# Block-sparse attention and a feed-forward layer in one kernel: q, k and v handed over in the operands' layout

## The chip, the cores and the metric

The kernel runs on one core of a Trainium2 chip. The metric is the device time of one execution in microseconds (us). Before the change three runs took 1019.51 us in the median (1017.39 to 1022.18).

## What is computed

The reference is attention over blocks of 32 positions with a mask, followed by a layer of the feed-forward kind (FFN). There are 4 batches of 8 heads, 768 positions and a head dimension of 64.

```python
scores = scale * np.matmul(q, k.transpose(0, 1, 3, 2))
# a pair of blocks is allowed when it is within the window, in a first or last row or column, or sampled
scores = np.where(mask, scores, -1000000000.0)
scores = scores - np.max(scores, axis=-1, keepdims=True)
attn = np.exp(scores)
attn = attn / (np.sum(attn, axis=-1, keepdims=True) + 1e-09)
x = np.matmul(attn, v)          # heads side by side: 3072 tokens of 512
h = x @ w_in                    # 512 to 2048
g = h - np.tanh(h)
out = g @ w_out                 # 2048 to 512
```

## The kernel before

**Precision.** Every float32 operand of a product is split into a high part that TensorE takes in its reduced float32 form and a low part that is the rest, and a product is the sum of three products of parts.

**The attention** goes over 16 pairs of heads (`pr`), two heads `h` of a pair, and six tiles of 128 keys (`kt`) of each head, so over 192 key tiles. For each pair, k and q are loaded in the order of the reference, with 128 partitions of positions (`load`, line 123). TensorE must contract over the head dimension, so `prep_qk` (line 178) transposes them: 6 transposes of 128x128 for k and 6 for q (line 186) into a buffer `pt` in PSUM. ScalarE copies the high part `hi` out of it (line 188), and VectorE subtracts it from the transposed values, which gives the low part `lo` (line 189). `dist` (line 192) then spreads the parts by DMA into one of three slots, 12 transfers for a pair (line 201). A slot holds four operands of the scores: sA (high k, mask, ones), sB (high q, one-hot blocks, minus the row maximum), sC (low k over high k) and sD (high q over low q).

For each key tile there are two products. `smax` (line 238) makes approximate scores `sm` from the high parts (line 245), and VectorE reduces them to row maxima `mc` (line 246). After six of them `smax_fin` (line 248) transposes the maxima on TensorE (`pmt`, line 251), VectorE turns them into `nm` (line 253), and a DMA writes `nm` as the last row of sB (line 254). `qk_exp` (line 263) then makes the scores `st` in full (lines 269 and 270; line 270 reads the row of `nm`), and ScalarE takes the exponential `pe` (line 272). `split` (line 275) splits it into `ph` (ScalarE, line 282, one in twelve on VectorE) and `pl` (GpSimd, line 284, one in twelve on VectorE). `accum` (line 288) multiplies them with v (lines 299, 305 and 306, 18 short products for a tile). `prep_v` (line 208) scales and splits v: VectorE finds its largest value (line 212), ScalarE writes the high part (line 230), VectorE the low one (line 231). `norm` divides by the row sums, and `spill` writes the result of a pair to DRAM.

`sm`, `st` and `pt` share three PSUM buffers (`big`), and `pmt`, `av` and the small transposes of `prep_v` share two (`one`).

**The order.** Each step is entered in a list with a time in key tiles (`at`, line 332) and emitted in the order of these times. `TQK = -15.1` puts the preparation of k and q 15.1 tiles ahead of the pair's first `st`, `TSM = -10.3` puts `smax` 10.3 tiles ahead. This order is only a priority. A list scheduler then sets the order on each engine, and takes a later step first where the one ahead of it isn't ready by its own reckoning. On the chip each engine, and SP's queue of DMA issues, works strictly in the order that came out.

**The first pair** goes the same way as the others: load, transposes, copies, 12 transfers. `fill` (line 169) writes mask and one-hot rows into the slots by DMA. `urgent` and `after` keep less urgent transfers behind those of the first pair.

**The FFN** (class `FFN`, line 441) goes over chunks of tokens and 16 tiles of the 2048 hidden columns. Its weights lie in DRAM as 64-bit floats; `convert` (line 411) makes float32 of a tile by three VectorE instructions (lines 415, 418, 421). The first three tiles of both weights are fetched and converted during the attention (`load_pre` and `convert_pre`, lines 358 and 364, at times `W0 + DW * x`) and go back to DRAM.

## Time and profile before

| what | us |
|---|---|
| three runs, median (range) | 1019.51 (1017.39 to 1022.18) |
| span of the profiled execution | 1019.9 |
| its start, up to the first product `st` of full scores | 27.98 |
| pair 0, from there to the first `st` of pair 1 | 29.91 |
| pair 1 | 36.19 |
| pairs 2 to 14 (13 pairs) | 320.92 |
| pair 15, to the end of its last `st` | 18.40 |
| the rest: last `accum` and FFN | 586.50 |

The profile gives no time of the profiled execution besides its span, which lies within the three runs. In the profile PE is TensorE's products and PEld its weight loads, DVE is VectorE, ACT ScalarE, POOL GpSimd, SP the queue that issues the DMAs. A row of the timeline has the start and the length in us, the engine, the line of the kernel, the operation and the tiles it writes and reads. PEclk is the clock that TensorE was granted, as a share of the full one.

### The profile page before, as it was taken

What the parts mean: (1) busy time and instruction counts of PE and PEld (TensorE: products, weight loads), DVE (VectorE), ACT (ScalarE), POOL (GpSimd) and SP (SyncE); (2) the same over time, 40 slices, a digit from 0 to 9 for tenths busy, and PEclk for the clock granted to TensorE, in tenths of its full rate; (3) what the DMA queues carried; (4) which work ended last, traced back from release to release, by engine and by line L of the source; (5) the groups of instructions that cost most, each with busy time, mean ns of one, the idle gap of its engine ahead of it and who ended that gap; (6) DMA issues with size and microseconds to landing.
All of it is one profiled execution on the core that took longest, in us unless ns stands there. A gap on an engine that the chain in (4) does not pass through costs nothing.

```text
span 1019.9 us, 19428 instructions
## 1 busy us (share of the span) xinstructions
PE 948.4 (93%) x7472; PEld 795.2 (78%) x7472; DVE 786.0 (77%) x1261; ACT 590.9 (58%) x926; POOL 637.0 (62%) x436
## 2 busy tenths in 40 slices
PE   5888999999999999897888899999999999999997
PEld 3667877888788888785766678888888888888896
DVE  5689887878788888979899987666666756666676
ACT  1665887888888888744344444445444534543453
POOL 1564777777778777866877866545455544544554
PEclk9997999999999999999899999999999999999999
DMA  7987687777766757133233121011000100000010
GB/s 193 252 223 205 144 175 151 157 173 169 159 157 156 156 131 183 48 120 105 81 114 92 43 93 52 1 42 42 21 5 17 63 1 1 31 11 1 1 42 22
DMA packets 73549, 97.75 MB, mean 96 GB/s; under 512 B 5880, under 2 KB 63416, under 8 KB 73456
## 3 DMA queue, kind: packets, MB, share of 16 engines
q1 hardware_dynamic: 73456, 96.51, 37.4%
q8 instruction: 59, 0.97, 0.4%
q14 instruction: 34, 0.28, 0.1%
HBM read 43.59 MB, written 14.16 MB: 57 GB/s over the span
## 4 chain that ended last, share of the span: by engine, by line
PE 64%; DVE 18%; DMA 8%; issue 5%; ACT 2%; POOL 1%; SPq 1%; POOLq 0%; DVEq 0%; ACTq 0%
PE h L507 21%; PE o L545 7%; PE o L543 7%; PE o L544 7%; PE st L269 5%; PE sm L245 5%; PE st L270 4%; DMA slot<-hiq 4%; PE av L299 2%; DVE g L524 2%; PE av L306 2%; PE av L305 2%; DMA slot<-nm 2%; DVE rs L316 2%; DVE mc L246 2%
## 5 line engine op out<-in xcount | busy, mean ns | idle before, releaser
L284 POOL TENSOR_TENSOR pl<-pe,ph 128x768 f16<-128x768 f32 x173 | 294.8, 1721 | 132.6 <-ACT ph L282 98.1
L530 POOL TENSOR_TENSOR gl<-g,gh 128x512 fp32r<-128x512 f32 (+2 forms) x112 | 135.1, 1209 | 191.6 <-ACT gh L529 191.3
L246 DVE TENSOR_REDUCE mc<-sm 128x1 f32<-128x768 f32 x192 | 181.6, 950 | 49.6 <-PE sm L245 48.4
L272 ACT ACTIVATE pe<-st 128x768 f32<-128x768 f32 x192 | 154.4, 805 | 77.3 <-PE st L270 72.8
L529 ACT ACTIVATE gh<-g 128x512 fp32r<-128x512 f32 (+2 forms) x112 | 63.9, 571 | 219.8 <-DVE g L526 210.6
L520 POOL TENSOR_SCALAR mk<-u 128x512 f32<-128x512 f32 (+2 forms) x112 | 160.9, 1436 | 46.6 <-ACT u L514 39.8
L522 DVE TENSOR_TENSOR g<-h,u 128x512 f32<-128x512 f32 (+2 forms) x112 | 68.4, 611 | 127.1 <-ACT t L516 115.8
L269 PE MATMUL st<-slot 128*128 128x512 f32 (+1 forms) x384 | 145.4, 379 | 8.8 <-DVE mc L246 4.8
L282 ACT ACTIVATE ph<-pe 128x768 f16<-128x768 f32 x168 | 141.7, 843 | 4.5
L270 PE MATMUL st<-slot 89*128 89x512 f32 (+1 forms) x384 | 128.7, 355 | 4.9 <-DMA slot<-nm 4.9
L299 PE MATMUL av<-vhl,ph 128*128 128x65 f16 x1152 | 130.2, 195 | 0.6 <-DVE sc L220 0.6
L245 PE MATMUL sm<-slot 88*128 88x512 f32 (+1 forms) x384 | 114.6, 385 | 16.7 <-DMA slot<-hiq 12.5
L305 PE MATMUL av<-vhl,ph 128*128 128x64 f16 x1152 | 130.0, 196 | 0.0
L306 PE MATMUL av<-vhl,pl 128*128 128x65 f16 x1152 | 128.2, 194 | 0.1
L306 PEld LDWEIGHTS <-pl 128*128 128x128 f16 x1152 | 107.9, 100 | 10.8 <-issue 6.8
L299 PEld LDWEIGHTS <-ph 128*128 128x128 f16 x1152 | 108.3, 98 | 4.6 <-issue 1.1
L305 PEld LDWEIGHTS <-ph 128*128 128x128 f16 x1152 | 108.9, 98 | 2.3 <-issue 1.6
L543 PE MATMUL o<-wx,gh 128*128 128x512 f32 x240 | 96.0, 400 | 7.9 <-ACT gh L529 6.9
L507 PE MATMUL h<-slot,wx 128*128 128x384 f32 (+1 forms) x480 | 102.5, 363 | 0.5 <-DVE t L523 0.5
L269 PEld LDWEIGHTS st<-slot 128*128 128x128 f32 x384 | 76.0, 198 | 28.9 <-DVE mc L246 7.4
L545 PE MATMUL o<-wx,gl 128*128 128x512 f32 x240 | 92.0, 398 | 4.9 <-POOL gl L530 4.7
L514 ACT ACTIVATE u<-h 128x512 f32<-128x512 f32 (+2 forms) x112 | 59.7, 533 | 62.8 <-PE h L507 52.4
(108 smaller groups left out, 2021.8 us busy)
## 6 DMA issues: line engine op xcount, KB each, us to landing
slot<-hik SPq DMA_DIRECT2D x64, 192.0 KB
slot<-hiq SPq DMA_DIRECT2D x64, 192.0 KB
stage<-w_in SPq DMA_DIRECT2D x13, 512.0 KB
stage<-w_out SPq DMA_DIRECT2D x13, 512.0 KB
rawk<-k SPq DMA_DIRECT2D x16, 384.0 KB
rawq<-q SPq DMA_DIRECT2D x16, 384.0 KB
slot<-lok SPq DMA_DIRECT2D x32, 192.0 KB
slot<-loq SPq DMA_DIRECT2D x32, 192.0 KB
```

Source lines behind the costliest of these rows:

```text
L245: nc.tensor.matmul(pm[:, c], lhsT=sB[s][0:88, j, t * P : (t + 1) * P], rhs=sA[s][0:88, j, c], start=True, stop=True)
L246: nc.vector.tensor_reduce(out=mcs[h][:, t : t + 1], in_=pm[:, 0:S], op=ALU.max, axis=AX.X)
L269: nc.tensor.matmul(st[:, c], lhsT=sC[s][:, j, kc], rhs=sD[s][:, j, c], start=True, stop=False)
L270: nc.tensor.matmul(st[:, c], lhsT=sA[s][0:89, j, kc], rhs=sB[s][0:89, j, c], start=False, stop=True)
L284: d = eng.tensor_tensor(out=pl, in0=pe, in1=ph, op=ALU.subtract)
L299: m = nc.tensor.matmul(o[:, to, :], lhsT=ph[:, c], rhs=vv[:, 0:65], start=(kt == 0 and t == 0), stop=False, skip_group_check=True)
L305: nc.tensor.matmul(o[:, to, 0:64], lhsT=ph[:, c], rhs=vv[:, 65:129], start=False, stop=False, skip_group_check=True)
L306: nc.tensor.matmul(o[:, to, :], lhsT=pl[:, c], rhs=vv[:, 0:65], start=False, stop=last, skip_group_check=True)
L507: nc.tensor.matmul(ph, lhsT=w[:, cc], rhs=x[:, c, tk], start=(k == 0), stop=(k == 3 * NCT - 1))
L520: nc.gpsimd.tensor_scalar(out=mk, in0=u, scalar1=THR2, scalar2=None, op0=ALU.is_gt)
L543: nc.tensor.matmul(o, lhsT=gh[:, c], rhs=wo[0][ft], start=(ft == 0), stop=False)
L545: nc.tensor.matmul(o, lhsT=gl[:, c], rhs=wo[0][ft], start=False, stop=(ft == NFT - 1))
```

## The change

- numpy now hands over k and q with the head dimension on the partitions, the two heads of a pair side by side and the two halves of 384 positions on the upper and lower 64 partitions. v comes with 128 positions on the partitions. The loads are plain copies of 128 rows of 768 values, as many bytes as before.
- `prep_qk` has no transposes and no PSUM buffer: ScalarE copies `hi` from the loaded tile, and VectorE subtracts `hi` from the loaded tile. `dist` is as it was, for pairs 1 to 15.
- Positions stand in natural order, so the table `TORD` is gone, and output rows are written in order.
- The first pair's operands are no longer spread by `dist`. `load_first` loads k and q of pair 0 twice, on both halves of the partitions (8 transfers of 192 KB). `first_high` and `first_low` write the slot's parts by ScalarE (8 copies), GpSimd and VectorE (2 subtractions each). Mask and one-hot rows of the first slot are written by VectorE (head 0) and GpSimd (head 1). The small constants come through ScalarE's DMA queue, and so do the rows `nm` of heads 0 and 1.
- The first weights have later times: `W0` goes from 40 to 52, the step `DW` from 24.7 to 23.5, and the conversion from 4 to 12 key tiles behind its load.

```diff
-W0, DW = 40, 24.7
+W0, DW = 52, 23.5
...
     def load(pr, which="kqv", first=None):
-        b, hp = divmod(pr, H // 2)
-        r = loads.setdefault(pr, [])
+        r = loads.setdefault(pr, {})
         for nm, src in ((n, x) for n, x in (("k", k), ("q", q), ("v", v)) if n in which):
-            t = p2.tile([P, 2, T, D], F32, tag="raw" + nm, name=f"raw{nm}{pr}", bufs=3 if nm == "v" else 2)
-            d = nc.sync.dma_start(out=t, in_=src[b, 2 * hp : 2 * hp + 2].rearrange("h (p t) d -> p h t d", t=T))
-            r.append(t)
+            r[nm] = p2.tile([P, 2, HS], F32, tag="raw" + nm, name=f"raw{nm}{pr}", bufs=3 if nm == "v" else 2)
+            d = nc.sync.dma_start(out=r[nm], in_=src[pr])
             if pr <= 3 and first is not None:
                 after(first, d)
-    load(0, "kq")
+    M = slice(64, 88)
+    twice = [[p2.tile([P, S], F32, tag="pe", name=f"twice{nm}{j}", bufs=4) for nm in "kq"] for j in range(2)]
+    def load_first():
+        for j in range(2):
+            for half in range(2):
+                for src, dst in zip((k, q), twice[j]):
+                    d = nc.sync.dma_start(
+                        out=dst[64 * half : 64 * half + 64, :].rearrange("d (r c) -> d r c", r=2),
+                        in_=src[0, :, j * HS : (j + 1) * HS].rearrange("(r d) c -> d r c", r=2),
+                    )
+                    urgent[0].append(d)
+    def first_high(j):
+        for x, dst in enumerate((sA, sB)):
+            nc.scalar.activation(out=dst[0][0:64, j], in_=twice[j][x][0:64], func=AF.Copy)
+    def first_low(j):
+        kk, qq = twice[j]
+        nc.scalar.activation(out=sC[0][64:128, j], in_=kk[64:128], func=AF.Copy)
+        nc.scalar.activation(out=sD[0][0:64, j], in_=qq[0:64], func=AF.Copy)
+        nc.gpsimd.tensor_tensor(out=sC[0][0:64, j], in0=kk[0:64], in1=sA[0].bitcast(F32)[0:64, j], op=ALU.subtract)
+        nc.vector.tensor_tensor(out=sD[0][64:128, j], in0=qq[0:64], in1=sB[0].bitcast(F32)[0:64, j], op=ALU.subtract)
+    oh = acst.tile([P, S], F32, name="oh")
     def setup():
+        sp_i = acst.tile([P, 6], I32, name="sp_i")
+        nc.scalar.dma_start(out=sp_i[M, :], in_=samp)
...
+        nc.scalar.dma_start(out=st_sb[M, :], in_=blocks[:, 0 : 2 * NB])
+        nc.scalar.dma_start(out=oh[M, :], in_=blocks[:, 2 * NB :])
...
+        for j, eng in enumerate((nc.vector, nc.gpsimd)):
+            eng.tensor_copy(out=sB[0][M, j], in_=oh[M, :])
+            eng.tensor_copy(
+                out=sA[0][M, j].rearrange("p (n c) -> p n c", c=BLK), in_=neg[M, :].unsqueeze(2).to_broadcast([NB, NB, BLK])
+            )
+        make_identity(nc, ident)
+        nc.vector.memset(qbias, QB)
...
-    def fill(i, dst, src, first=None):
-        R = slice(64, 88)
-        d = nc.sync.dma_start(out=dst[i].bitcast(F32)[R], in_=src[R, :].unsqueeze(1).to_broadcast([NB, 2, S]))
-        if first is not None:
-            after(first, d)
+    def fill(i):
+        after(0, nc.sync.dma_start(out=sB[i].bitcast(F32)[M], in_=oh[M, :].unsqueeze(1).to_broadcast([NB, 2, S])))
+        after(0, nc.sync.dma_start(out=sA[i].bitcast(F32)[M], in_=sA[0].bitcast(F32)[M]))
     def prep_qk(pr, nm):
-        raw = loads[pr][0 if nm == "k" else 1]
+        raw = loads[pr][nm]
         hi = p2.tile([P, 2, HS], F32R, tag="hi" + nm, name=f"hi{nm}{pr}", bufs=1)
-        lo = p2.tile([P, 2 * HS], F32R, tag="lo" + nm, name=f"lo{nm}{pr}", bufs=1).rearrange("p (j c) -> p j c", j=2)
-        pt = big(f"pt{nm}{pr}")
-        for j in range(2):
-            for u in range(3):
-                c = (3 * j + u) * P
-                nc.tensor.transpose(pt[:, c : c + P], raw[:, j, 2 * u : 2 * u + 2, :].rearrange("p r d -> p (r d)"), ident)
-        ptv = pt[:, 0:S].rearrange("p (j c) -> p j c", j=2)
-        nc.scalar.activation(out=hi, in_=ptv, func=AF.Copy)
-        nc.vector.tensor_tensor(out=lo, in0=ptv, in1=hi.bitcast(F32), op=ALU.subtract)
+        lo = p2.tile([P, 2, HS], F32R, tag="lo" + nm, name=f"lo{nm}{pr}", bufs=1)
+        nc.scalar.activation(out=hi, in_=raw, func=AF.Copy)
+        nc.vector.tensor_tensor(out=lo, in0=raw, in1=hi.bitcast(F32), op=ALU.subtract)
         hl[pr, nm] = hi, lo
     def dist(pr, nm, part):
...
-                if pr == 0:
-                    urgent[part].append(d)
...
-        rv = loads[pr][2]
-        vf = rv.rearrange("p h t d -> p (h t) d")
+        rv = loads[pr]["v"]
+        vf = rv.rearrange("p h (t d) -> p (h t) d", d=D)
...
-        d = nc.sync.dma_start(
+        d = (nc.scalar if h < NMH else nc.sync).dma_start(
...
-        vv = vhl[pr % NV][:, j, TORD[kt], :]
+        vv = vhl[pr % NV][:, j, kt, :]
...
-    onehot, mask = setup()
+    load_first()
+    setup()
...
-    at(-17.0, fill, 0, sB, onehot)
-    at(TQK + 0.3, fill, 0, sA, mask, 0)
-    at(TQK + 0.9, load, 1, "kq", 0)
-    at(TQK + 1.7, load, 0, "v", 1)
+    for j in range(2):
+        at(TSM - 0.5 + 3 * j, first_high, j)
+        at(TSM + 1 + 3 * j, first_low, j)
+    at(TSM - 0.2, load, 1, "kq", 0)
+    at(TSM - 0.1, load, 0, "v", 0)
     for i in range(1, NSLOT):
-        for dst, src in ((sB, onehot), (sA, mask)):
-            at(TQK + TF * i, fill, i, dst, src, 1)
+        at(TSM + TF * i, fill, i)
...
-        for nm, dt in (("k", 0), ("q", 0.5)):
+        for nm, dt in (("k", 0), ("q", 0.5)) if pr else ():
...
-        at(W0 + DW * x + 4, convert_pre, "io"[x % 2], x // 2)
+        at(W0 + DW * x + 12, convert_pre, "io"[x % 2], x // 2)
...
-                nc.sync.dma_start(out=out[b * S : (b + 1) * S, :].rearrange("(p t) d -> t p d", t=T)[t], in_=ob)
+                nc.sync.dma_start(out=out[(b * T + t) * P : (b * T + t + 1) * P, :], in_=ob)
...
-    block = (col % P * T + np.array(TORD)[col // P]) // BLK
+    block = col // BLK
...
+    def turned(a):
+        a = np.asarray(a).reshape(NPAIR, 2, 2, HS, D)
+        return a.transpose(0, 2, 4, 1, 3).reshape(NPAIR, P, 2 * HS)
...
-        "q": inputs["q"],
-        "k": inputs["k"],
-        "v": inputs["v"],
+        "q": turned(inputs["q"]),
+        "k": turned(inputs["k"]),
+        "v": np.asarray(inputs["v"]).reshape(NPAIR, 2, T, P, D).transpose(0, 3, 1, 2, 4).reshape(NPAIR, P, 2 * HS),
```

The list scheduler makes a new order of all this. From the end of the attention on (the last 3235 TensorE instructions, the last 706 of VectorE and 539 of ScalarE) the order is that of before. Three places differ in what the prediction speaks of. In the rows, a number behind a name is that of the pair or head, and of the tile behind it: `nm16` belongs to head 16, `hik10` to pair 10, `st13_2` to tile 2 of head 13. Pair p has the heads 2p and 2p+1.

**VectorE at the start, before**, from the first maximum `mc` of head 0 (`mc0`) over `nm` of head 0 to the first low part of pair 1:

```order
L246 TENSOR_REDUCE mc0_172<-sm0_0_173 128x1
L246 TENSOR_REDUCE mc0_172<-sm0_1_177 128x1
L246 TENSOR_REDUCE mc0_172<-sm0_2_181 128x1
L246 TENSOR_REDUCE mc0_172<-sm0_3_185 128x1
L246 TENSOR_REDUCE mc0_172<-sm0_4_189 128x1
L246 TENSOR_REDUCE mc0_172<-sm0_5_193 128x1
L246 TENSOR_REDUCE mc1_217<-sm1_0_218 128x1
L246 TENSOR_REDUCE mc1_217<-sm1_1_222 128x1
L253 TENSOR_SCALAR nm0_199<-pmt0_197 6x128
L246 TENSOR_REDUCE mc1_217<-sm1_2_226 128x1
L212 TENSOR_REDUCE am0_202<-rawv0_166 128x1
L189 TENSOR_TENSOR lok1_231<-ptk1_232,hik1_230 128x768
```

and **after**, from the third maximum of head 0 to `nm0`; `L151` is the low part of q for head 1, `L197` the low parts of pair 1, `L218` the largest value of v:

```order
L252 TENSOR_REDUCE mc0_143<-sm0_2_158 128x1
L151 TENSOR_TENSOR slot0_72<-twiceq1_97,slot0_72 64x768
L252 TENSOR_REDUCE mc0_143<-sm0_3_164 128x1
L252 TENSOR_REDUCE mc0_143<-sm0_4_174 128x1
L197 TENSOR_TENSOR lok1_216<-rawk1_137,hik1_215 128x768
L252 TENSOR_REDUCE mc0_143<-sm0_5_178 128x1
L197 TENSOR_TENSOR loq1_222<-rawq1_139,hiq1_221 128x768
L218 TENSOR_REDUCE am0_187<-rawv0_141 128x1
L252 TENSOR_REDUCE mc1_202<-sm1_0_203 128x1
L252 TENSOR_REDUCE mc1_202<-sm1_1_207 128x1
L259 TENSOR_SCALAR nm0_184<-pmt0_182 6x128
```

The low parts of pair 1 and the reduction of v moved from behind `nm0` to ahead of it. The low parts of pair 0 (two subtractions ahead of all maxima before) became one ahead of them and one between them.

**ScalarE, where it copies the high parts of pair 8 (line 188), before**:

```order
L282 ACTIVATE ph13_1_3409<-pe13_1_3327 128x768
L272 ACTIVATE pe13_2_3379<-st13_2_3374 128x768
L282 ACTIVATE ph13_2_3483<-pe13_2_3379 128x768
L188 ACTIVATE hik8_3389<-ptk8_3391 128x768
L272 ACTIVATE pe13_3_3407<-st13_3_3402 128x768
L188 ACTIVATE hiq8_3455<-ptq8_3457 128x768
L282 ACTIVATE ph13_3_3502<-pe13_3_3407 128x768
```

and **after** (line 196):

```order
L278 ACTIVATE pe10_0_2487<-st10_0_2482 128x768
L288 ACTIVATE ph10_0_2561<-pe10_0_2487 128x768
L278 ACTIVATE pe10_1_2507<-st10_1_2502 128x768
L196 ACTIVATE hik8_3271<-rawk8_2698 128x768
L288 ACTIVATE ph10_1_2576<-pe10_1_2507 128x768
L278 ACTIVATE pe10_2_2559<-st10_2_2554 128x768
L196 ACTIVATE hiq8_3330<-rawq8_2700 128x768
```

The copies of pair 8 moved from the exponentials of head 13 to those of head 10, by 19 key tiles. They no longer wait for TensorE, and the subtractions on VectorE moved along.

**SP, one pair's transfers into its slot, before**:

```order
L128 DMA rawv11_4246<-v 128x2x384
L254 DMA slot2_79<-nm16_3798 1x6x128
L128 DMA rawk11_4242<-k 128x2x384
L201 DMA slot0_77<-hik9_3868 64x2x384 x3
L201 DMA slot0_77<-hiq9_3934 64x2x384 x2
L201 DMA slot0_77<-hik9_3868 64x2x384
L201 DMA slot0_77<-lok9_3869 64x2x384 x2
L201 DMA slot0_77<-hiq9_3934 64x2x384 x2
L201 DMA slot0_77<-loq9_3935 64x2x384 x2
L128 DMA rawq11_4244<-q 128x2x384
L254 DMA slot2_79<-nm17_4048 1x6x128
```

and **after**:

```order
L328 DMA xscr1_61<-xq6_3324 768x1x128
L209 DMA slot1_73<-hik10_4204 64x2x384 x2
L209 DMA slot1_73<-lok10_4205 64x2x384
L260 DMA slot2_74<-nm16_3669 1x6x128
L209 DMA slot1_73<-hik10_4204 64x2x384
L209 DMA slot1_73<-hiq10_4263 64x2x384 x2
L124 DMA rawv11_4100<-v 128x768
L209 DMA slot1_73<-hik10_4204 64x2x384
L209 DMA slot1_73<-lok10_4205 64x2x384
L209 DMA slot1_73<-hiq10_4263 64x2x384 x2
L209 DMA slot1_73<-loq10_4264 64x2x384 x2
L260 DMA slot2_74<-nm17_3900 1x6x128
```

Before, the row `nm` of the even head (`nm16`) stood ahead of all 12 transfers of a pair, and that of the odd head (`nm17`) behind them. After, `nm16` stands behind the first three of them. They go to the slot that pair 7 used: those three wait until tile 2 of head 15 is done with the first half of its columns, and the others until tile 5 is.

More of the change, by code (lines that the diff above doesn't have):

```diff
@@ L297, in accum @@
             last = kt == T - 1 and t == T - 1
-            to = TORD[t]
-            m = nc.tensor.matmul(o[:, to, :], lhsT=ph[:, c], rhs=vv[:, 0:65], start=(kt == 0 and t == 0), stop=False, skip_group_check=True)
+            m = nc.tensor.matmul(o[:, t, :], lhsT=ph[:, c], rhs=vv[:, 0:65], start=(kt == 0 and t == 0), stop=False, skip_group_check=True)
             if t == 0 and kt % 2 == 0 and PAIR:
@@ L304, in accum @@
                 )
-            nc.tensor.matmul(o[:, to, 0:64], lhsT=ph[:, c], rhs=vv[:, 65:129], start=False, stop=False, skip_group_check=True)
-            nc.tensor.matmul(o[:, to, :], lhsT=pl[:, c], rhs=vv[:, 0:65], start=False, stop=last, skip_group_check=True)
+            nc.tensor.matmul(o[:, t, 0:64], lhsT=ph[:, c], rhs=vv[:, 65:129], start=False, stop=False, skip_group_check=True)
+            nc.tensor.matmul(o[:, t, :], lhsT=pl[:, c], rhs=vv[:, 0:65], start=False, stop=last, skip_group_check=True)
     def norm(h):
```

51 lines of the change are left out of this document (16 added, 35 removed).

## The prediction

> **What bounds the kernel now.** The page first: it gives the span and the busiest engine.
>
> ```profile
> span 1019.9 us, 19428 instructions
> PE 948.4 (93%) x7472; PEld 795.2 (78%) x7472; DVE 786.0 (77%) x1261; ACT 590.9 (58%) x926; POOL 637.0 (62%) x436
> ```
>
> A share over the whole says little here, so I cut the span into stages (the windows: PE, PEld, DVE, ACT and POOL busy, granted clock, DMA share, GB/s). The cuts are the first `st` products of pairs 0, 1 and 2 and of pair 15, and the end of the last `st`.
>
> ```profile
> 0.00:27.98 27.98, 13.89 (x46) 10.05 (x47) 15.28 (x28) 4.53 (x5) 4.70 (x9) 1.00 0.81 193
> 27.98:57.89 29.91, 27.83 (x270) 22.90 (x270) 21.61 (x38) 20.05 (x26) 19.11 (x11) 1.00 0.89 238
> 57.89:94.08 36.19, 30.02 (x306) 24.71 (x307) 32.75 (x48) 21.62 (x27) 20.08 (x11) 0.80 0.79 215
> 94.08:415.00 320.92, 303.90 (x3970) 262.57 (x3970) 269.15 (x453) 266.84 (x340) 240.67 (x144) 0.99 0.70 159
> 415.00:433.40 18.40, 16.20 (x217) 14.14 (x214) 17.92 (x21) 15.00 (x24) 15.76 (x10) 1.00 0.14 43
> 433.40:1019.90 586.50, 556.56 (x2677) 460.85 (x2674) 429.29 (x678) 262.83 (x509) 336.70 (x253) 0.99 0.14 44
> ```
>
> The fourth row is the steady state, and the products of its `st` count its pairs.
>
> ```profile
> L269 PE MATMUL st<-slot x312: 280/392/629, 94.1 to 412.9; 128*128 128x512 f32 x156
> ```
>
> A pair has 12 key tiles of two such products, so 312 are 13 pairs: 320.92 / 13 = 24.69 us a pair, of which PE is busy 303.90 / 13 = 23.38, VectorE 20.70, ScalarE 20.53, GpSimd 18.51. TensorE bounds this stage at 95%, and 1.31 us a pair are holes. The largest named wait of its products in this stage is for the high parts of q (us, times, longest):
>
> ```profile
> PE sm L245 <- DMA slot<-hiq: 7.3, 6, 2.1
> ```
>
> The start is another matter. The chain of waits runs there over transfers, and the timeline shows what they hold up.
>
> ```profile
> 16.62 6.13 DMA slot<-hiq
> 22.85 7.08 DMA slot<-nm
> 29.97 0.80 PE st L270
> ```
>
> ```profile
> 0.73 0.45 SPq L128 DMA_DIRECT2D rawk<-k  x1
> 6.54 1.29 PEld L186 LDWEIGHTS ptq<-ident,rawq 128*128 128x128 f32 x6
> 7.00 0.81 ACT L188 ACTIVATE hik<-ptk 128x768 fp32r<-128x768 f32 x1 [4.99 <-PE ptk L186]
> 13.46 6.52 PE L245 MATMUL sm<-slot 88*128 88x512 f32 x16 [5.22 <-DMA slot<-hiq]
> 14.50 7.01 DVE L246 TENSOR_REDUCE mc<-sm 128x1 f32<-128x768 f32 x8 [3.45 <-PE sm L245]
> 21.43 0.27 DVE L253 TENSOR_SCALAR nm<-pmt 6x128 fp32r<-6x128 f32 x1
> ```
>
> The row `nm` of head 0 is ready at 21.7 us, is issued at 22.85 and lands only at 29.93, behind the transfers that SP had issued before it. The full scores wait for it.
>
> **The change, part by part.** The sum is made against the span of 1019.9, which is 0.4 us from the median of the three runs.
>
> *Start.* Before, the first `sm` needs load, transposes, a copy and two transfers (13.46). After, it needs four loads of 192 KB, two copies and the mask. Before, the same 768 KB had landed by 6.54, when q's transposes began without a wait. Two copies of 0.81 make 8.2: the first `sm` is 5.3 us earlier. Up to `nm0` VectorE then has, by the order, 8 maxima, two L151, two L197 and the reduction of v: 13 operations of about 0.9 (7.01 / 8 = 0.88 for a maximum, the subtractions 0.95 below) are 11.7. So `nm0` is made at about 20.5, only 1 us earlier, but with 2.9 us of pair 1's work done. It now goes by ScalarE's queue. Its flight there is not in the trace; the bounds are 0.75 us for the issue alone (below) and 7.08 with SP's backlog. I take 2.5, nearer the low end, since nothing stands ahead of it in its own queue but three transfers of the first microseconds: landing at 23.5 instead of 29.93, **6.5 us** (4 to 8.5). The Trainium skill, "DMA: Bandwidth & Descriptors", section "Queues, rings and completion order", says that each DMA engine goes round the queues that have work, packet by packet; by that `nm0` passes the backlog, which agrees with the low end, and no run here shows it yet. The eight loads, 1.5 MB, take the place of 0.8 MB of loads and 2.3 MB of spreading, so the queue is emptier. GpSimd's share of the setup hides behind ScalarE's eight copies of 0.81; uncovered it would cost a subtraction or two of the 1.65 us below.
>
> *Pair 0.* TensorE is busy 27.83 of 29.91. The 12 transposes for pair 2 leave: I take **1.5 us** (0 to 3), from these rows, where the transposes run in the steady state at 211.97 and 214.08, and the next product begins 0.66 and 0.69 us after each six begin:
>
> ```profile
> 211.97 0.82 PE L186 MATMUL ptk<-ident,rawk 128*128 128x128 f32 x6
> 212.63 0.19 PE L306 MATMUL av<-vhl,pl 128*128 128x65 f16 x1
> 214.08 0.85 PE L186 MATMUL ptq<-ident,rawq 128*128 128x128 f32 x6
> 214.77 0.19 PE L306 MATMUL av<-vhl,pl 128*128 128x65 f16 x1
> ```
>
> That is 1.35 us of TensorE a pair.
>
> *Pair 1.* It takes 36.19 and is VectorE's: 32.75 busy (90%), with the conversion of the first weights in it and the clock at 0.80.
>
> ```profile
> 67.61 0.94 DVE L246 TENSOR_REDUCE mc<-sm 128x1 f32<-128x768 f32 x1
> 71.15 0.43 DVE L415 TENSOR_SCALAR cvti<-rawi 128x512 int32<-128x512 int32 x1 [2.59 <-DMA rawi<-w_in]
> 72.43 1.88 DVE L418 SCALAR_TENSOR_TENSOR cvti<-rawi,cvti 128x512 int32<-128x512 int32 x1
> 74.23 1.87 DVE L415 TENSOR_SCALAR cvto<-rawo 128x512 int32<-128x512 int32 x1
> ```
>
> The later times of the change do little: the second tile's conversion, which waits 2.59 us for its load here, stands behind 29 maxima instead of 27, and the first behind 19 instead of 20. The wait should go, two key tiles being some 4 us; the conversions stay in this pair. Taking 32.75 and VectorE's 0.6 more (below) at 97%, as in the fifth row, the pair would take 34.4: **2 us** less, with +1 to -7 as bounds, since I can't say where the clock falls.
>
> *Pairs 2 to 14.* TensorE needs 23.38 - 1.35 = 22.03 us a pair. `hi` and `lo` come 19 key tiles earlier, so the wait for q goes. VectorE gets dearer, because the subtraction now reads two SBUF tiles where one was in PSUM. The rows of the old subtraction, of an operation with two SBUF inputs (min/median/max in ns), and of GpSimd's:
>
> ```profile
> L189 DVE TENSOR_TENSOR lok<-ptk,hik x16: 903/947/957, 9.2 to 384.0; 128x768 fp32r<-128x768 f32 x16
> L231 DVE SCALAR_TENSOR_TENSOR vhl<-rawv,sb,vhl x16: 970/1270/1703, 40.2 to 403.4; 128x768 f16<-128x768 f32 x16
> L284 POOL TENSOR_TENSOR pl<-pe,ph x173: 1636/1652/2420, 33.0 to 437.2; 128x768 f16<-128x768 f32 x173
> ```
>
> So 0.32 us more each (0.0 to 0.76), 0.64 a pair: VectorE needs 21.34. Two engines at 22.03 and 21.34 in fixed orders don't run without holes. In the third and fifth row VectorE bounds at 90.5% and 97.4%; the middle, 94%, gives 22.7, and I take 22.8: (24.69 - 22.8) x 13 = **24.6 us** (14, at 23.6 a pair, to 30, at 22.4). The Trainium skill, "SBUF — State Buffer", section "SBUF: two separate sides", says that such an operation and a GpSimd one exclude each other for a whole instruction. By that, with GpSimd busy 75% of this stage, an estimate is 0.75 x 1.65 / 2 = 0.62 us for each subtraction, and VectorE's need about 21.9; the spread of 970 to 1703 agrees with such a lock.
>
> ScalarE's copies take 0.81 from PSUM; from SBUF I take the same. The freed PSUM buffer is a gain that I don't count apart.
>
> *The rest.* Pair 15 has no transposes in it, and the FFN's order is unchanged, as are its operations: 0 (2 either way). Loads, v's parts and output rows move as many bytes in as many transfers.
>
> Sum: 6.5 + 1.5 + 2 + 24.6 = 34.6, and 1019.9 - 34.6 = **985 us**.
>
> **The rivals.**
>
> *VectorE takes over.* At the longest time of L231 the subtractions add 1.5 us a pair, VectorE needs 22.2, above TensorE's 22.03, and at 94% a pair takes 23.7. The gain there is 13 us, and the whole 1019.9 - 23 = 997. For it speaks how near the two are, and the lock of the SBUF page; against it that pl's 1652 is close to its shortest, so that the collisions are few.
>
> *TensorE stays the bound without holes.* 22.03 a pair gives 34.6 there and, with the other terms at their values, 975. For it: the middle stage already runs at 95% with the wait for q in it. Against: VectorE would be at 97%.
>
> *Slower: the even heads wait for `nm`.* By SP's order `nm16` now stands behind three transfers of 192 KB that wait for a slot. A row `nm` behind such a backlog takes from issue to landing:
>
> ```profile
> 126.56 5.65 DMA slot<-nm
> 38.32 0.75 SPq L254 DMA_DIRECT2D slot<-nm  x1
> ```
>
> (the lower row is an issue alone). From `nm`'s transpose to the product that needs it, TensorE has two `sm`, one `st` and most of three `accum` to do by the order, about 3.5 us by these rows (an `sm` takes 0.42 to the next start, an `st` 0.71, an `accum` 0.62):
>
> ```profile
> 203.99 0.59 PE L245 MATMUL sm<-slot 88*128 88x512 f32 x2
> 204.41 0.40 PE L269 MATMUL st<-slot 128*128 128x512 f32 x1
> 205.12 0.21 PE L299 MATMUL av<-vhl,ph 128*128 128x65 f16 x1
> 205.74 0.59 PE L245 MATMUL sm<-slot 88*128 88x512 f32 x2
> ```
>
> At 5.65, with 0.5 for the transpose and `nm`, each pair waits 2.6 us. After such a hole the clock has halved:
>
> ```profile
> 170.00:175.20 5.20, 3.12 (x49) 2.64 (x48) 2.50 (x3) 3.41 (x5) 3.26 (x3) 1.00 1.09 224
> 175.20:178.60 3.40, 3.40 (x22) 2.92 (x21) 2.29 (x7) 2.10 (x3) 0.57 (x2) 0.50 1.11 214
> ```
>
> 3.4 us at half are 1.7 more, so 13 x 4.3 = 56, and 985 + 56 = 1041. It decides from a flight of 3.0 us on. Against it: the three transfers start at tile 2, two tiles ahead of `nm16`, and have mostly landed by then.
>
> *The change doesn't do what it says* for the weights: their order hardly moves, which is in the sum of pair 1.
>
> **How the numbers follow.** Forecast 0.60, VectorE 0.20, no holes 0.10, the wait for `nm` 0.06, and 0.04 for that wait at some 60% of its price, which cancels the gain. All terms at their best give 971, at their worst 1003; I give 968 to 1004, which holds the first three cases, about 0.9 of the chance, less what I misjudge in their bounds. 0.5%, 5 us, is about what a measurement of this kernel can tell from no change. Faster 0.90, same 0.04, slower 0.06.
>
> **What would show it.** In the changed kernel's windows a pair of the middle should take 22.8 us, with TensorE at 97% and VectorE at 94%; the subtractions' median should be 1.0 to 1.5 us. The first `nm` should land near 23.5, and no wait for `hiq` should be left. I am wrong if waits for `nm` in even heads are among the longest, if VectorE is above 97% in the middle, or if the FFN's 586.5 us move.

## The result, and the profile after

The changed kernel takes 1067.92 us in the median of four runs (1065.26 to 1071.65), the kernel before 1020.85 beside it (1017.39 to 1025.74, four runs): a ratio of 1.0465 with a 95% interval of 1.0428 to 1.0502. It is slower by 47 us; I had forecast 35 us faster.

The page of the changed kernel, span and engines:

```profile
span 1066.3 us, 18966 instructions
PE 955.6 (90%) x7280; PEld 789.0 (74%) x7280; DVE 807.4 (76%) x1260; ACT 589.9 (55%) x932; POOL 645.6 (61%) x440
```

Its windows, cut as before at the first `st` of pairs 0, 1 and 2, then at those of pairs 13, 14 and 15 and at the end of the last `st`:

```profile
0.00:21.30 21.30, 9.07 (x23) 5.24 (x23) 17.97 (x26) 9.48 (x11) 11.21 (x13) 1.00 0.94 214
21.30:54.60 33.30, 25.35 (x242) 19.84 (x242) 23.93 (x37) 20.41 (x27) 19.40 (x11) 1.00 0.90 220
54.60:91.10 36.50, 27.95 (x284) 21.75 (x280) 31.47 (x54) 21.28 (x28) 19.69 (x12) 0.86 0.99 268
91.10:412.60 321.50, 273.03 (x3234) 229.05 (x3234) 242.84 (x380) 222.28 (x287) 205.32 (x121) 0.88 0.56 135
412.60:435.10 22.50, 22.48 (x310) 19.07 (x306) 19.03 (x33) 18.57 (x25) 18.16 (x11) 1.00 0.40 97
...
479.40:1066.30 586.90, 556.98 (x2678) 459.37 (x2676) 431.57 (x678) 262.80 (x509) 334.74 (x253) 0.99 0.13 44
```

Pairs 2 to 14 end at 461.1 and take 370.0 us, 28.5 a pair, where they took 320.9, 24.7 a pair. No engine is busier there: in pairs 2 to 12 (the fourth row) TensorE is at 85%, VectorE at 76%. The granted clock fell from 0.99 to 0.88. Pair 13, in which no copy for a later pair is left, takes 22.5. So the loss comes with the preparation of a later pair, and it is waiting. The waits in that fourth stage (us, times, longest), of ScalarE, VectorE and TensorE:

```profile
ACT hik L196 <- DMA slot<-hik: 28.3, 9, 5.6
...
DVE lok L197 <- ACT hik L196: 28.5, 9, 5.0
...
DVE loq L197 <- DMA slot<-loq: 7.5, 6, 2.4
...
PE st L275 <- DVE mc L252: 24.8, 11, 3.7
PE sm L251 <- ACT pe L278: 20.7, 15, 2.8
```

The first three were not in the trace of before; there `st` waited 3.5 us for `mc` and `sm` 0.2 us for `pe`. Two are waits for transfers that still read a buffer, the first and, smaller, that of `loq`; the timeline below shows how the others follow from the first. The order on ScalarE shows where pair 8's copy stood, before (first three rows) and now (last three):

```
179 L272 ACTIVATE pe13_2_3379<-st13_2_3374 128x768
180 L282 ACTIVATE ph13_2_3483<-pe13_2_3379 128x768
181 L188 ACTIVATE hik8_3389<-ptk8_3391 128x768
...
152 L278 ACTIVATE pe10_1_2507<-st10_1_2502 128x768
153 L196 ACTIVATE hik8_3271<-rawk8_2698 128x768
154 L288 ACTIVATE ph10_1_2576<-pe10_1_2507 128x768
```

It went from tile 2 of head 13 to tile 1 of head 10, from 16 to 35 tiles ahead of its pair. There is one buffer `hik`, and until their transfers have landed it holds the values of the pair before. The longest case, in the timeline of pair 3 (pair 6's copy; ScalarE, VectorE, TensorE, then SP's queue):

```profile
120.37 0.81 ACT L278 ACTIVATE pe<-st 128x768 f32<-128x768 f32 x1
126.80 0.84 ACT L196 ACTIVATE hik<-rawk 128x768 fp32r<-128x768 f32 x1 [5.62 <-DMA slot<-hik]
...
127.93 0.96 DVE L197 TENSOR_TENSOR lok<-rawk,hik 128x768 fp32r<-128x768 f32 x1 [4.98 <-ACT hik L196]
...
128.43 0.20 PE L304 MATMUL av<-vhl,ph 128*128 128x65 f16 x1 [4.14 <-ACT ph L288]
...
120.43 0.61 SPq L209 DMA_DIRECT2D slot<-hik  x1
```

and in its chain of waits:

```profile
120.43 6.35 DMA slot<-hik
```

SP issues the last transfer that reads pair 5's `hik` at 120.43. It lands 6.35 us later, at 126.78, and 0.02 us after that the copy for pair 6 starts. All that time ScalarE stands, with `ph` and `pe` of the present pair behind the copy; VectorE stands at `lok`, with the maxima behind it; TensorE runs dry. Then the clock halves:

```profile
128.90:135.70 6.80, 6.57 (x41) 5.42 (x42) 6.18 (x10) 4.84 (x8) 5.34 (x4) 0.50 0.62 176
```

A mean clock of 0.88 over 321.5 us, between 1.00 and this 0.50, is some 77 us at half speed, so by an estimate from these rows up to 38 us of the 49 are the slow clock behind the holes (less some 3 us that before lost in this way, at its mean of 0.99), and the rest the holes.

The start kept only part of its gain. The row `nm` of head 0 left by ScalarE's own queue:

```profile
21.81 0.79 ACTq L260 DMA_DIRECT2D slot<-nm  x1
...
28.94 0.79 PE L276 MATMUL st<-slot 89*128 89x512 f32 x1 [4.77 <-DMA slot<-nm]
```

7.1 us from issue to the product that waited for it. The twelve transfers of pair 1 were on the way: SP issued them from 12.7 us on, since this pair's copies had moved forward too, and the last two about when `nm` was issued.

### The profile page after: what moved, and what is told of

Its sections match the earlier page's. It is cut to its first block, busy times and chain, and to the rows that moved or that the text cites. A ratio compares the mean times of both kernels' runs of the same rounds, so it can differ in the third digit from the quotient of the medians.

```text
span 1066.3 us, 18966 instructions
## 1 busy us (share of the span) xinstructions
PE 955.6 (90%) x7280; PEld 789.0 (74%) x7280; DVE 807.4 (76%) x1260; ACT 589.9 (55%) x932; POOL 645.6 (61%) x440
## 4 chain that ended last, share of the span: by engine, by line
PE 56%; DVE 22%; DMA 10%; issue 5%; SPq 4%; ACT 1%; POOL 1%; POOLq 0%; ACTq 0%; DVEq 0%
PE h L513 19%; PE o L551 6%; PE o L549 6%; PE o L550 6%; PE st L275 4%; PE sm L251 4%; DMA slot<-loq 4%; PE st L276 4%; SPq L209 4%; DVE mc L252 3%; DVE g L530 3%; DVE g L531 2%; PE av L304 2%; DVE rs L321 2%; PE av L311 2%
## 5 line engine op out<-in xcount | busy, mean ns | idle before, releaser
L290 POOL TENSOR_TENSOR pl<-pe,ph 128x768 f16<-128x768 f32 x173 | 298.9, 1737 | 167.5 <-ACT ph L288 113.6
L275 PE MATMUL st<-slot 128*128 128x512 f32 (+1 forms) x384 | 154.5, 403 | 29.4 <-DVE mc L252 27.7
L251 PE MATMUL sm<-slot 88*128 88x512 f32 (+1 forms) x384 | 123.9, 410 | 33.7 <-ACT pe L278 21.6
L304 PE MATMUL av<-vhl,ph 128*128 128x65 f16 x1152 | 142.6, 200 | 6.4 <-ACT ph L288 4.1
L310 PE MATMUL av<-vhl,ph 128*128 128x64 f16 x1152 | 141.6, 200 | 0.1
L311 PE MATMUL av<-vhl,pl 128*128 128x65 f16 x1152 | 140.6, 199 | 0.7 <-POOL pl L290 0.4
L276 PE MATMUL st<-slot 89*128 89x512 f32 (+1 forms) x384 | 132.5, 365 | 4.8 <-DMA slot<-nm 4.8
L304 PEld LDWEIGHTS <-ph 128*128 128x128 f16 x1152 | 112.7, 101 | 14.6 <-issue 7.2
L311 PEld LDWEIGHTS <-pl 128*128 128x128 f16 x1152 | 112.0, 103 | 13.3 <-issue 6.1
L310 PEld LDWEIGHTS <-ph 128*128 128x128 f16 x1152 | 113.1, 102 | 4.6 <-issue 2.8
L251 PEld LDWEIGHTS sm<-slot 88*128 88x128 f32 x384 | 67.2, 218 | 41.8 <-ACT pe L278 25.9
```

The costliest lines, as they stand in the source:

```text
L251: nc.tensor.matmul(pm[:, c], lhsT=sB[s][0:88, j, t * P : (t + 1) * P], rhs=sA[s][0:88, j, c], start=True, stop=True)
L275: nc.tensor.matmul(st[:, c], lhsT=sC[s][:, j, kc], rhs=sD[s][:, j, c], start=True, stop=False)
L276: nc.tensor.matmul(st[:, c], lhsT=sA[s][0:89, j, kc], rhs=sB[s][0:89, j, c], start=False, stop=True)
L290: d = eng.tensor_tensor(out=pl, in0=pe, in1=ph, op=ALU.subtract)
L304: m = nc.tensor.matmul(o[:, t, :], lhsT=ph[:, c], rhs=vv[:, 0:65], start=(kt == 0 and t == 0), stop=False, skip_group_check=True)
L310: nc.tensor.matmul(o[:, t, 0:64], lhsT=ph[:, c], rhs=vv[:, 65:129], start=False, stop=False, skip_group_check=True)
```

## The experiments

My theory after the result (theory 1): the copies `hi` and subtractions `lo` stand too early in the order and block their engines. The rival (theory 2): another part of the change slows the pairs, and these waits only go along with it.

All kernels are edits of the changed kernel unless said otherwise. Ratios are to the kernel before, run on the same chip beside them (1020.85 to 1023.59 us). The stages come from the first `st` of each pair in each timeline.

| kernel | median us | ratio (95%) | to pair 1 | pair 1 | pairs 2-14 | after last `st` |
|---|---|---|---|---|---|---|
| before | 1020.85 | | 57.9 | 36.2 | 320.9 | 586.5 |
| after | 1067.92 | 1.0465 (1.0428-1.0502) | 54.6 | 36.5 | 370.0 | 586.9 |
| hold16 | 1043.74 | 1.0223 (1.0184-1.0262) | 55.8 | 34.1 | 345.3 | 586.1 |
| hold28 | 1022.22 | 1.0005 (0.9974-1.0035) | 54.7 | 39.3 | 323.0 | 584.6 |
| all2 | 1046.71 | 1.0259 (1.022-1.0298) | 56.7 | 33.8 | 348.0 | 588.4 |
| tback | 1017.37 | 0.9941 (0.9908-0.9973) | 53.2 | 35.9 | 325.1 | 586.3 |
| hold16a | 1013.09 | 0.9889 (0.9848-0.993) | 56.1 | 24.6 | 325.8 | 586.6 |
| w40 | 1012.77 | 0.9915 (0.9888-0.9941) | 56.4 | 24.6 | 329.2 | 584.7 |
| h28rs | 1016.12 | 0.993 (0.9905-0.9954) | 55.4 | 36.1 | 315.2 | 594.2 |
| h16arsn | 1014.26 | 0.9898 (0.9847-0.9949) | 44.7 | 31.5 | 321.9 | 596.1 |
| nolo | 1005.64 | 0.9842 (0.9786-0.9898) | 49.7 | 33.7 | 308.8 | 595.3 |
| before_rs | 1008.52 | 0.9847 (0.9806-0.9887) | 60.3 | 32.7 | 300.7 | 594.9 |
| tbrs | 1002.17 | 0.98 (0.9757-0.9843) | 51.5 | 34.7 | 306.0 | 595.7 |
| tbrsa | 1000.37 | 0.9787 (0.9746-0.9828) | 48.1 | 32.1 | 301.1 | 595.7 |
| tbrsa26 | 993.33 | 0.9716 (0.9673-0.976) | 51.3 | 31.8 | 304.1 | 584.8 |

**Hold the copies where they were (hold16).**

```diff
-        nc.scalar.activation(out=hi, in_=raw, func=AF.Copy)
+        d = nc.scalar.activation(out=hi, in_=raw, func=AF.Copy)
+        i = 12 * pr - (16 if nm == "k" else 15)
+        if i >= 0:
+            tc.add_manual_dep(
+                d.ins, pex[i].ins.name,
+                mybir.DependencyInfo(mybir.DependencyClass.NoSync, mybir.DependencyReason.DATA), reason="hold",
+            )
```

`pex[i]` is the exponential of key tile `i`. It runs on the same engine, so only the order is set.

> The changed kernel, with each `hik` and `hiq` on ScalarE held behind the exponential 16 and 15 key tiles ahead of its pair's first `st`, which is where they stood before the change. Nothing else is touched. Theory 1 (the copies `hi` and the subtractions `lo` now stand 35 tiles ahead, where the transfers that still read the one `hi` and `lo` buffer have only just started, and everything behind them on ScalarE and VectorE waits): no wait of ScalarE for `slot<-hik` is left, the middle goes from 28.5 to about 22.8 us a pair, and the whole is 985 us (975 to 1000). Theory 2 (the slower pairs come from something else in the change: VectorE's subtraction from SBUF, the loads in the new layout, SP's order, the row `nm`): the middle stays at 27 to 29 us a pair and the whole is 1045 to 1068.

Measured 1043.74: neither theory's number. The wait for `slot<-hik` is gone, and half of the loss with it, but two others stand at its place (the waits of the middle, VectorE and TensorE):

```profile
DVE am L225 <- DMA rawv<-v: 13.1, 9, 2.4
...
PE st L282 <- DVE sc L233: 13.6, 9, 2.5
```

`am`, the first step on v, was taken some 20 tiles ahead in every kernel up to here, counted in the maxima on VectorE. In this one SP's order has the load of raw v behind the 12 transfers, so VectorE now stands at `am`.

**Hold them only 7 tiles later (hold28).** The same edit with 28 and 27.

> As the kernel with the copies held, but 28 and 27 key tiles ahead, which is 7 tiles later than in the changed kernel and 12 earlier than before the change. The 12 transfers of the pair ahead need about 11 us from the start of their slot, and 8 tiles are some 15 us, so they have landed by then. Theory 1: the wait is gone here too, and the whole is within 10 us of the kernel held at 16 (980 to 1000). Theory 1b (any preparation earlier than before costs something, since it brings SP's transfers forward): between the two, 1000 to 1040. Theory 2: 1045 to 1068.

Measured 1022.22, 46 us less than the changed kernel. 7 tiles later is enough, and that the copies come 12 tiles earlier than before the change does no harm that shows in the middle (323.0 against 320.9). But theory 1's 980 to 1000 is missed: without blocking, the kernel is only as fast as before the change. The time lies in the range of theory 1b; against 1b, hold16a below has its copies where they stood before, and its middle is no shorter (325.8). The timeline shows the kind of wait that is left, VectorE ahead of a hole of TensorE, and GpSimd:

```profile
219.60 2.00 DVE L204 TENSOR_TENSOR loq<-rawq,hiq 128x768 fp32r<-128x768 f32 x1
221.52 1.60 DVE L328 TENSOR_SCALAR rs<-rs,sb 128x6 f32<-128x6 f32 x1
...
219.14 3.96 POOL L297 TENSOR_TENSOR pl<-pe,ph 128x768 f16<-128x768 f32 x2 [1.21 <-PE sm L258]
...
224.04 0.50 PE L282 MATMUL st<-slot 128*128 128x512 f32 x1 [2.29 <-DVE mc L259]
```

A product of six elements a partition takes 1.60 us, a subtraction 2.00. Durations in the middle (min/median/max in ns), here and, in the second fence, of the same product in the kernel before:

```profile
L204 DVE TENSOR_TENSOR loq<-rawq,hiq x12: 903/1152/1998, 93.9 to 362.9; 128x768 fp32r<-128x768 f32 x12
L204 DVE TENSOR_TENSOR lok<-rawk,hik x11: 935/935/2374, 115.7 to 361.9; 128x768 fp32r<-128x768 f32 x11
L328 DVE TENSOR_SCALAR rs<-rs,sb x27: 222/1141/1637, 102.9 to 424.2; 128x6 f32<-128x6 f32 x27
```

```profile
L316 DVE TENSOR_SCALAR rs<-rs,sb x26: 209/440/1700, 101.9 to 410.2; 128x6 f32<-128x6 f32 x26
```

Before the change the subtraction read PSUM and never took over 0.958 us. From SBUF 15 of the 23 take 0.90 to 0.95, and eight 1.40 to 2.37. Laid beside GpSimd's instructions in the same trace, each of the eight began while a `pl` was running and ended 0.82 us after it. Of the 27 small products 26 began while a GpSimd instruction was running and ended 0.03 us after it. Where a `pl` began beside a running subtraction, it was the `pl` that took longer, 2.2 to 2.7 us instead of 1.65. The Trainium skill, "SBUF — State Buffer", section "SBUF: two separate sides", says that VectorE and GpSimd share a pair of ports that one of them holds for a whole instruction; these rows agree.

**Two buffers instead of an order (all2).** The lines that make room for them are left out here.

```diff
-        hi = p2.tile([P, 2, HS], F32R, tag="hi" + nm, name=f"hi{nm}{pr}", bufs=1)
-        lo = p2.tile([P, 2, HS], F32R, tag="lo" + nm, name=f"lo{nm}{pr}", bufs=1)
+        hi = p2.tile([P, 2, HS], F32R, tag="hi" + nm, name=f"hi{nm}{pr}", bufs=2)
+        lo = p2.tile([P, 2, HS], F32R, tag="lo" + nm, name=f"lo{nm}{pr}", bufs=2)
```

> The changed kernel with two buffers each for `hik`, `hiq`, `lok` and `loq` instead of one. The room for them is taken from others: one buffer for the raw first weights instead of two, two for raw v instead of three, seven each for `ph` and `pl` instead of eight. By its order the copies move one more pair ahead, so that `hik` of pair p+4 stands at tile 1 of pair p, where the transfers of pair p+2, which read the buffer that it needs, have just started. Theory 1 as I hold it (the place in the order decides, not the number of buffers): the same waits of about 3 us a pair return and the whole is 1050 to 1075. Theory 1c (one buffer is the cause, a second one cures it): 980 to 1000.

Measured 1046.71, 3 us under theory 1's range and far from a cure. The wait is back, at two thirds of its size:

```profile
ACT hik L196 <- DMA slot<-hik: 18.1, 9, 4.7
```

A second buffer lets the scheduler go one pair further ahead, to the same point in the pair, where the transfers that read the buffer have only just begun. It is the order that costs, and a buffer alone doesn't mend it. Not all of the loss here is this wait: the room was taken from other buffers, and `am` waits 11.3 us for the load of v, which has one buffer less.

**The transposes back (tback).**

```diff
-        nc.scalar.activation(out=hi, in_=raw, func=AF.Copy)
-        nc.vector.tensor_tensor(out=lo, in0=raw, in1=hi.bitcast(F32), op=ALU.subtract)
+        pt = big(f"pt{nm}{pr}")
+        for j in range(2):
+            for u in range(3):
+                c = (3 * j + u) * P
+                nc.tensor.transpose(pt[:, c : c + P], raw[:, j, u * P : (u + 1) * P], ident)
+        ptv = pt[:, 0:S].rearrange("p (j c) -> p j c", j=2)
+        nc.scalar.activation(out=hi, in_=ptv, func=AF.Copy)
+        nc.vector.tensor_tensor(out=lo, in0=ptv, in1=hi.bitcast(F32), op=ALU.subtract)
```

> The changed kernel with 12 TensorE transposes a pair put back for pairs 1 to 15: `hi` and `lo` are made from a PSUM buffer again, as before the change. What is transposed are the tiles that numpy has already turned, so the scores are those of other values; the number and shape of all operations are those of the kernel before. Start, weights, layout of loads and natural order stay as changed. By its order `hik` stands 16 tiles ahead again. Theory 1: 1013 us, which is the 1019.9 of before less the 6.7 us that the start gained (1005 to 1020). Theory 2, by which the loss lies in another part of the change: 1040 or more.

Measured 1017.37, in the range of theory 1. Start, layout, natural order and weights together cost nothing; the whole loss came with the transposes' going. What had kept `hik` at its place were the transposes and their buffer `pt` in PSUM, which it has to wait for in the scheduler's order too.

**Hold `am` as well (hold16a).** hold16, and:

```diff
+        if pr > 1:
+            tc.add_manual_dep(
+                d.ins, mci[12 * pr - 10].ins.name,
+                mybir.DependencyInfo(mybir.DependencyClass.NoSync, mybir.DependencyReason.DATA), reason="hold",
+            )
```

`d` is the reduction `am`, `mci[i]` the maximum `mc` of key tile `i`.

> The kernel with `hi` held at 16 and 15 tiles, and now also the reduction `am` of raw v held on VectorE behind the maximum 10 tiles ahead of the pair (it stood 21 ahead). Theory 1, widened (a step that the order takes too early blocks its engine; in the held kernel `am` waits 13.1 us in the middle for `rawv`, whose load stands behind the 12 transfers): the wait for `rawv` goes, and the middle falls from 345 to 323 us, the whole from 1044 to 1020 (1012 to 1028). Theory 3 (the held kernel is slow for VectorE's dearer subtraction from SBUF, and the wait for `rawv` lies beside it): the whole stays at 1035 to 1044.

Measured 1013.09. The middle is 325.8 as expected, and `am` waits no more. 10 us more come from pair 1, which I hadn't expected. Part of it only moved: by the windows VectorE is busy 24.0 us there instead of hold16's 31.5, and 31.9 instead of 26.2 in pair 2. The granted clock of pair 1 rose from 0.79 to 0.97. Why the order came out so stays open. This is the change with its order mended: 1.1% faster than before the change.

**The weights' times (w40).** hold16a with `W0, DW = 40, 24.7` and `+ 4`.

> The kernel with `hi` held at 16 and `am` at 10 tiles, and the times of the first weights as before the change (40, 24.7, conversion 4 behind). If these times matter as little as I forecast: within 4 us of the same kernel with the later times, 1009 to 1017. If the later times are what makes its pair 1 short (24.6 us; 36.2 before): pair 1 is 33 to 37 and the whole 1018 or more.

Measured 1012.77: no difference. That pair 1 takes 24.6 in both says that the later times aren't why it is short.

**The small product off VectorE (h28rs, before_rs).** hold28, and the kernel before, with:

```diff
-        nc.vector.tensor_scalar(out=rs, in0=rs, scalar1=sbs[pr][:, 1:2], scalar2=None, op0=ALU.mult)
-        nc.vector.tensor_tensor(
-            out=xq[pr][:, :, j, :], in0=o[:, :, 0:64], in1=rs.unsqueeze(2).to_broadcast([P, T, D]), op=ALU.mult
-        )
+        nc.vector.scalar_tensor_tensor(
+            out=xq[pr][:, :, j, :], in0=o[:, :, 0:64], scalar=sbs[pr][:, 1:2],
+            in1=rs.unsqueeze(2).to_broadcast([P, T, D]), op0=ALU.mult, op1=ALU.mult,
+        )
```

> The kernel with `hi` held at 28 and 27 tiles, and the small product `rs` by `sb` of each head (128x6, median 1.14 us in the middle, 0.22 at its shortest) taken off VectorE: the product of `av` and `rs` that follows takes the factor `sb`, a power of two, as its scalar. Theory L (what is left there is VectorE standing still beside GpSimd's `pl` with operands in SBUF, and TensorE waiting 13.5 us for `mc`): VectorE loses 27 x 1.07 = 29 us of work in the middle, the waits for `mc` fall below 5 us, a pair takes 23.0 to 23.5, and the whole is 1000 us (990 to 1010). Rival (the fixed orders and the transfers set the rest): 1015 to 1022.

> The kernel before, with the same small product taken off VectorE. TensorE bounds it at 95% of the middle and its products wait 3.5 us for `mc` there. Theory: at most these 3.5 us and one hole each are gained, 1015 us (1008 to 1021). If VectorE was a hidden bound of the kernel before as well: 1005 or less.

h28rs: 1016.12, a miss. The middle falls by 8 us, not 20, and 10 come on after the attention. before_rs: 1008.52, within the first range, but the stages say the other thing: its middle falls by 20.2 us, and 8.4 come on after the attention. A steady pair of before and of before_rs (the windows):

```profile
293.31:316.77 23.46, 23.05 (x312) 19.98 (x308) 20.68 (x35) 20.65 (x27) 18.66 (x12) 1.00 0.68 158
```

```profile
302.35:324.82 22.47, 22.47 (x312) 19.86 (x308) 19.11 (x33) 20.06 (x27) 18.24 (x12) 1.00 0.73 177
```

With all its transposes TensorE does a pair in 22.47 us without a hole. The 23.05 of before, for the same products at the same clock, and the 23.38 a pair of its whole middle are thus not what TensorE needs. The records of successive products overlap (in the prediction's rows the product at 212.63 begins before the 0.82 us of those at 211.97 are over), so a short delay between two products counts as busy. Whether it was VectorE's standing still or the scheduler's new order around it that made the difference, these two kernels don't tell apart.

**All together (h16arsn), and without the subtractions (nolo).** h16arsn is hold16a with the small product gone and pair 1's copies held behind the issue of head 0's `nm`; nolo is that with `lo` left out:

```diff
-        lo = p2.tile([P, 2, HS], F32R, tag="lo" + nm, name=f"lo{nm}{pr}", bufs=1)
+        lo = lozero[nm]
...
-        nc.vector.tensor_tensor(out=lo, in0=raw, in1=hi.bitcast(F32), op=ALU.subtract)
```

> All together on the changed kernel: `hi` held at 16 and 15 tiles, `am` at 10, the small product gone from VectorE, and pair 1's copies held behind the issue of head 0's `nm`. Before that last hold the 12 transfers of pair 1 were queued ahead of `nm`, which was issued at 21.8 and landed at 28.9; by it `nm` is to land near 23.5, and the first full scores come 5 us earlier. With a middle of 23.0 to 23.5 us a pair (299 to 306) in place of 370: the whole is 990 us (980 to 1005). If the transfers held back only come due later, pair 1 gives the start's gain back: 995 to 1005. If VectorE's subtractions still bound the middle: 1005 to 1015.

> The kernel with all holds and without the small product, and now without the subtractions `lo` too: `dist` spreads a tile of zeros in their place, so the scores lack their low parts, which leaves out 2 of VectorE's operations a pair and nothing of TensorE's or of the transfers. Steady pairs take 23.5 us with them. F1 (TensorE's own need without transposes is 22.47 - 1.35 = 21.1 us, as I had it but for the size, and the subtractions hold it up): 21.2 to 21.8 us a pair, the whole 990. F2 (TensorE needs 22.4 with or without the transposes): 22.3 to 22.6 a pair, the whole 1001. F3 (the subtractions hold nothing up): 23.3 to 23.6, 1013.

h16arsn: 1014.26, missed by 24; it is in the range of the third case, by which VectorE's subtractions still bound the middle. What was expected of `nm` holds: with pair 1's transfers behind it, the same `nm` on the same queue takes 1.9 us instead of 7.1 to the product that needs it.

```profile
19.51 0.81 ACTq L273 DMA_DIRECT2D slot<-nm  x1
...
21.43 0.79 PE L289 MATMUL st<-slot 89*128 89x512 f32 x1
```

The stages up to pair 1 gain 11.4 us on hold16a. Pairs 1 and 2 (31.5 and 32.8, against 24.6 and 33.2) give 6.5 of them back, the steady pairs of the middle stay near 23.5, and the feed-forward layer takes 9.5 more. nolo: 1005.64. A steady pair of h16arsn and of nolo:

```profile
251.80:275.36 23.56, 22.42 (x294) 18.65 (x294) 21.46 (x33) 20.11 (x27) 19.83 (x12) 1.00 0.70 168
```

```profile
320.98:343.33 22.35, 22.00 (x296) 18.58 (x294) 18.15 (x30) 20.27 (x28) 18.68 (x12) 1.00 0.76 191
```

So the two subtractions from SBUF hold a steady pair up by 1.2 us, unless the new order around them has a part in it, and without them a pair without transposes still takes 22.2 to 22.4 where it is steady (four of the 13): F2 by the number of these pairs, with the whole 5 us above its 1001. Why TensorE doesn't get below 22.2 with 12 products less stays open; no engine but TensorE is above 91% in that row.

**The transposes back for good (tbrs, tbrsa, tbrsa26).** The edit of tback, with numpy handing pairs 1 to 15 over so that the transposes give the right operands, and the small product gone; tbrsa also holds `am`; tbrsa26 keeps the small product for heads 26 to 31.

> The changed start and layout, but the transposes put back for pairs 1 to 15 (numpy hands these pairs over so that the transposes give the right operands), and the small product `rs` by `sb` taken off VectorE. Theory (what the kernel before waited for in the middle was VectorE, so that TensorE has room for the transposes, and `lo` made from PSUM does not stand still beside GpSimd): the middle is that of the kernel before with the same edit, 300 us, the first three stages are some 5 us shorter, and the whole is 1003 us (996 to 1008). Rival (without the transposes is better once nothing blocks): 1010 or more.

> The same with `am` held at 10 tiles. If the early `am` blocks VectorE here as well (with the transposes put back it waited 4.1 us for `rawv` in the middle): 2 to 8 us below the same kernel without the hold. If not: within 2 us of it.

> The kernel with the transposes put back, `am` held and the small product gone, but the product left as it was for heads 26 to 31. All kernels without the product took 594 to 596 us after the last `st` instead of 586.5, and their orders in the feed-forward layer differ from before. With the last heads as they were, that part's order is before's again. If the order there costs the 8 us: 586 to 588 after the last `st`, the whole 992 (988 to 996). If they come from something else (the weights landing later against an earlier end of the attention): 594 again, and the whole 1000.

1002.17, 1000.37 and 993.33. A steady pair of tbrsa:

```profile
289.68:312.21 22.53, 22.53 (x312) 19.87 (x308) 19.57 (x33) 20.51 (x27) 18.64 (x12) 1.00 0.75 177
```

22.5 us with the transposes, against 23.5 without them in h16arsn, in which `am` and the small product are treated alike. The hold on `am` is worth 2 us, which these runs hardly resolve. With the last heads left alone the order in the feed-forward layer is that of before again, and it takes 584.8 instead of 595.7: the 11 us there were order, of which pair 14 gives 3.7 back (27.5 against 23.8) and pair 0 another 3.2 (28.9 against 25.7, at a granted clock of 0.82 against 1.00). At 0.9716 (0.9673 to 0.976) tbrsa26 beats both kernels.

## Why the prediction was wrong

- **The step that failed** is "`hi` and `lo` come 19 key tiles earlier, so the wait for q goes". I saw the move in the order, booked it as a gain and asked neither what the earlier copy has to wait for nor what is queued behind it. It needs the one `hi` buffer, whose readers are the transfers that start only when a slot comes free. The term was to be -24.6 us and was +49.1; hold28, hold16a and tback each take 44 to 47 of it away again. Nor was a gain of 24.6 behind the wait: with it gone the middle is 323.0 (hold28) and 325.8 (hold16a) against 320.9 before, for the next two reasons.
- **TensorE's need.** 23.38 less 1.35 was too simple: tbrsa does a pair with transposes in 22.53. Of the 0.85 in between some 0.2 is, by an estimate from the mean clock of 0.99, the slower clock; the rest is waiting that counted as busy. A steady pair with the transposes is only 0.1 to 0.3 us longer than one of nolo without them (22.53 against 22.2 to 22.4), not 1.35; what TensorE itself would need without them isn't shown.
- **VectorE's subtraction.** 0.32 us each was near: 0.36 for `loq` and 0.20 for `lok` in the means of hold28 (1.307 and 1.143 against 0.952 and 0.943). But what counts is that TensorE waits behind it: the two subtractions from SBUF hold a steady pair up by 1.2 us (h16arsn against nolo), and made from PSUM they leave TensorE without a hole (tbrsa). The rival "VectorE takes over" comes nearest to this mechanism, though VectorE's busy share of a steady pair is only 91% (h16arsn); it decides what is left when nothing blocks. In the changed kernel itself the medians were 0.96, below the 1.0 to 1.5 that I had given as a sign.
- **The start.** The first `sm` came at 9.1 (forecast 8.2) and `nm` was issued at 21.8; its flight, taken at 2.5 us, was 7.1, the upper bound that I had given. What I had drawn from the Trainium skill ("DMA: Bandwidth & Descriptors", "Queues, rings and completion order"), which says that each DMA engine takes the queues in turn, packet by packet, is not borne out: `nm` on a queue of its own did not pass the backlog, 7.1 us behind it and 1.9 ahead of it. What held it there isn't shown. Start and pair 0 gained 3.3 us, not 8.0.
- **Pair 1** gained nothing (36.5 for 36.2, forecast 34.2). **The rest** held: 586.9 for 586.5, and the weights' times are worth nothing (w40).
- **The rival that ended slower** had the right sign and the wrong mechanism, but for the halved clock behind the holes, which it priced and my sum did not. No product of the middle waits for a row `nm` to land. The queue that mattered was ScalarE's, not SP's.

Of my own signs, "no waits for `hiq` left" came true for TensorE but for 0.2 us, while ScalarE's own wait for the transfers was in no list of mine. None of my three signs of being wrong came: VectorE was at 76% in pairs 2 to 12, and the FFN took 586.9.

## What to carry to other kernels

When a change takes a resource away that a step had to wait for, look up where the scheduler puts the step then, and cost the wait that it meets there: on an engine that works in order, a step taken too early blocks all that is behind it. Ask for every moved step which buffer it writes and who still reads it; more buffers move the step again, an order that is pinned doesn't. And a busy TensorE is not a need: leave out what it waits for, as with the small product here, before an engine is called the bound.

## What the runs showed of the hardware

- A VectorE product of 128x6 from SBUF takes 0.21 us, and up to 1.70 beside GpSimd's `pl`, ending 0.03 us after the GpSimd instruction in which it began (26 of 27 in hold28); without it a pair of the kernel before ran in 22.5 instead of 23.5 us.
- A row of 3 KB on ScalarE's own DMA queue took 7.1 us behind the twelve transfers of 192 KB of pair 1 on SP's queue, and 1.9 with these held back.
- After holes of up to 4.1 us in TensorE, in the middle of the changed kernel, the clock stood at 0.50 for 3.4 to 10.2 us at a time.
